# LayerNorm rows turned by transposing DMAs, and one 1/sqrt chain for two norms, in a gMLP block's z stage

## The chip, the cores and the metric

The kernel runs on one core of one Trainium2 chip. The metric is the time of one execution on the device in microseconds (us); several runs are made and their median is taken. The profile is of one execution, by the hardware profiler. Its engines are PE (TensorE's matmuls), PEld (TensorE's weight loads, which overlap PE), DVE (VectorE), ACT (ScalarE), POOL (GpSimd) and SP (SyncE, which issues DMAs; SPq is its queue). Each engine works through its instructions in the order of the program and waits on semaphores for others.

## The reference

One sequence of S = 2048 rows of D = 512, float32. First an attention block of 32 heads with a LayerNorm ahead of it, then a gMLP block with a LayerNorm ahead of it:

```python
x = A_x
h = x + _A_ref(_layernorm(x), A_wqkv, A_wo)
h2 = h + _B_ref(_layernorm(h), B_w_in, B_w_sp, B_b_sp, B_w_out)
...
z = _gelu(jnp.einsum("bsd,df->bsf", x, w_in))
z1 = z[..., :Fh]
z2 = _layernorm(z[..., Fh:], axis=-1)
g = jnp.einsum("ts,bsf->btf", w_sp, z2) + b_sp[None, :, None]
return jnp.einsum("bsf,fd->bsd", z1 * g, w_out)
```

Fh is 688. What is computed to the end of the z stage is h, then z from the LayerNorm of h, then the LayerNorm of z's second half.

## The kernel before, in words

The kernel has four stages: the projections q, k and v; attention (the longest by far), in which POOL also prepares the weights of what follows; the z stage; and the last stage with the spatial product and the output. Matmuls take float16 parts: a float32 tile is split into a float16 high part and a float16 rest, and `mm3` (lines 106 to 109) multiplies high by high, high by rest and rest by high.

The z stage works on 16 blocks of 128 rows in the order `h_rows`: 0, 1, 8, 9, 2, 10, 3, 11 and so on. Its loop over k (from line 1243) is written out by hand, under a manual schedule: the order in the code is the order on each engine. In iteration k it does this, for the block `sb` = row[k] and the later block `new` = row[k + 2]:

- `make_h(new)`: twelve matmuls (L747) of the attention's output o with wo. DVE adds x (L751, in the tile xr, which holds x and then h), SP stores h (L752), DVE takes statistics (L754).
- `split_o(row[k + 3])`: o's float16 high part on ACT (L737) and its rest on DVE (L740).
- `make_z(sb, 1, ...)`: two quarters of z, the second half of its columns, twelve matmuls each (lines 107 to 109) with hT, the turned LayerNorm of h, as the stationary operand; the Gelu on ACT (L1192).
- `turn(row[k + 1])`, between these two: PE transposes the float32 tile hn in four 128 × 128 blocks into PSUM (L1177), ACT takes the high part (L98), DVE the rest (L104).
- `scale_h(new)`: DVE makes 1/sqrt of the variance of h by three Newton steps (`rstd_of`, lines 111 to 131), and `minus_mean` (L768); ACT then makes hn (L1271).
- Statistics of z's second half (L1265), then two more quarters, the first half of z's columns.
- `gate_z(sb)`: z's first half is stored from ACT's queue (L1209); a second 1/sqrt chain on DVE; ACT normalizes z's second half (L1214); then float16 parts of it and of sums and differences of blocks, on ACT, POOL and DVE (L1196, L1197, L1220 to L1236). For k = 13 this is put off into the next iteration.
- `meanwhile()`, inside `gate_z`: POOL multiplies the next o by the reciprocals rc (L731), and SP asks for the o, rc and x of row[k + 5] (`load_o`: four o, four rc, one xr; L723, L726, L729).

In the last eight iterations SP also fetches operands of the last stage (L1163, op).

Pools set how far work can run ahead: accumulators `acc` of the z stage have five PSUM banks and the transposes two; xr and hn have three buffers, o and rc two; z's second half has four, its first half one. In the attention stage, h of the first two blocks is made between the units of the scores, at fixed values of n, and the LayerNorm of the first block on DVE (`new_hn`, L764).

Of the kernel before, what the change touches and what calls it, by code (L numbers as in the profile page):

```python
# [59 lines left out]
def block_kernel(ctx: ExitStack, tc: tile.TileContext, x, wqkv, wo, w_in, w_sp4, b_sp, w_out, out):  # L60
# [652 lines left out]
    wi4 = w_in.rearrange("(a p) c -> p a c", p=P)  # L713

    h_rows = [0, 1, HB, HB + 1] + [sb + HB * i for sb in range(2, HB) for i in range(2)]
    os_, o2s, xrs, hns, hTs = {}, {}, {}, {}, {}

    def load_o(sb):

        c = slice(sb * P, (sb + 1) * P)  # L720
        o = e2.tile([P, DB, P], F32, name="o")
        for d in range(DB):
            nc.sync.dma_start(o[:, d, :], o_scr[d, :, :DH, c])  # L723
        rc = e2.tile([P, DB, P], F32, name="rc")
        for d in range(DB):
            nc.sync.dma_start(rc[:, d, :], r_scr[8 * d:8 * d + 8, c].rearrange(  # L726
                "h (o s) -> h o s", o=1).to_broadcast([8, DH, P]))
        xrs[sb] = e2.tile([P, D], F32, name="xr", bufs=3)
        nc.sync.dma_start(xrs[sb], x[c, :])  # L729
        os_[sb] = o  # L730
        return lambda: nc.gpsimd.tensor_mul(o, o, rc)  # L731

# [27 lines left out]

    def new_hn(sb):
        mv, rs = scale_h(sb)
        hns[sb] = e2.tile([P, D], F32, name="hn", bufs=3)
        nc.vector.tensor_scalar(hns[sb], xrs.pop(sb), mv[:, 0:1], rs, op0=ALU.subtract, op1=ALU.mult)  # L764

    def minus_mean(pool, mv, rs):
        nb = pool.tile([P, 1], F32, name="nb")
# [20 lines left out]
    with ExitStack() as at:  # L788
# [256 lines left out]
        for n in range(0, len(units), 2):  # L1045
# [85 lines left out]
                invert()  # L1131
            if n in (474, 484, 504, 508):
                asked.append(load_o(h_rows[{474: 0, 484: 1, 504: 2, 508: 3}[n]]))
            if n in (484, 492, 508):
                asked.pop(0)()
            if len(later) == 1 or n in (498, 510):
# [2 lines left out]
                steps_h.append(make_h(h_rows[1], later[0].tile([P, 512], F32, name="h")))  # L1139
            if n == 502:  # L1140
                new_hn(h_rows[0])
        weigh(*prev)
        take(*prev[:2], e2)
        asked.append(load_o(h_rows[4]))
# [21 lines left out]
    with ExitStack() as mid:  # L1166
        m2 = mid.enter_context(tc.tile_pool(name="mid_2", bufs=2))
        zs, zst = {}, {}
        ps = mid.enter_context(tc.tile_pool(name="mid_ps", bufs=5, space=PSUM))
        pt = mid.enter_context(tc.tile_pool(name="mid_pt", bufs=2, space=PSUM))  # L1170

        def turn(sb):

            hn = hns.pop(sb)
            tp = pt.tile([P, DB, P], F32, name="tp")
            for d in range(DB):
                nc.tensor.transpose(tp[:, d, :], hn[:, d * P:(d + 1) * P], ident)  # L1177
            hTs[sb] = [m2.tile([P, DB, P], F16, name=f"hT{i}") for i in range(2)]
            split(hTs[sb][0], hTs[sb][1], tp, "act")

        def new_z(sb):
            zs[sb] = [m2.tile([P, FH], F32, name=f"z{i}", bufs=1 + 3 * i) for i in range(2)]
            zst[sb] = m2.tile([P, 2, 6], F32, name="zst")

        def make_z(sb, i, c):

            hT, f = hTs[sb], slice(i * FH + c * FC, i * FH + (c + 1) * FC)
            acc = ps.tile([P, 512], F32, name="acc")
            for d in range(DB):
                mm3(acc[:, :FC], hT[0][:, d, :], hT[1][:, d, :],  # L1190
                    wi2[0][:, d, f], wi2[1][:, d, f], d == 0, d == DB - 1)
            nc.scalar.activation(zs[sb][i][:, c * FC:(c + 1) * FC], acc[:, :FC], AF.Gelu_apprx_tanh,  # L1192
                                 scale=gelu_down)

        def parts(name, k, src, eh, el):
            (nc.gpsimd.tensor_copy if eh == "pool" else nc.scalar.copy)(T[name][0][:, k, :], src)  # L1196
            sub = lambda e: e.tensor_sub(T[name][1][:, k, :], src, T[name][0][:, k, :])  # L1197
            if el == "later":
                subs.append(sub)
            else:  # L1200
                sub(nc.gpsimd if el == "pool" else nc.vector)

        subs, put_off = [], []

        def gate_z(sb, meanwhile):

            z = zs.pop(sb)
            rows = slice(sb * P, (sb + 1) * P)
            nc.scalar.dma_start(z_scr[rows, :], z[0])  # L1209
            mv = m2.tile([P, 2], F32, name="zmv")  # L1210
            nc.vector.bn_aggr(mv, zst.pop(sb))
            rs = rstd_of(m2, mv[:, 1:2], 1, up=Z2_UP)
            nb = minus_mean(m2, mv, rs)
            nc.scalar.activation(z[1], z[1], AF.Identity, bias=nb, scale=rs)  # L1214
            zs[sb] = z[1]
            meanwhile()
# [12 lines left out]
            t2 = m2.tile([P, FC], F32, name="t2", bufs=1)  # L1229
            e.tensor_sub(t2, b22, t1)  # L1230
            parts("t2", k, t2, eh, el)
            parts("b22", k, b22, "pool" if last else "act", "pool")
            nc.gpsimd.tensor_sub(b12, b22, b12)
            parts("t3", k, b12, "pool", "pool")
            parts("b21", k, b21, "pool" if last else "act", "pool" if last else "later")
            nc.gpsimd.tensor_sub(t2, b21, t2)  # L1236
            parts("n4", k, t2, "pool", "pool")

        row = dict(enumerate(h_rows))
        with tc.manual_schedule(engines={E.PE, E.Activation, E.DVE, E.Pool, E.SP}):  # L1240
            asked.pop(0)()
            turn(row[0])
            new_hn(row[1])
            for k in range(NB):
                sb, new = row[k], row.get(k + 2)
                if new is not None:
                    for _ in make_h(new, ps.tile([P, 512], F32, name="acc")):
                        pass
                if k + 3 < NB:
                    split_o(row[k + 3])  # L1250
                new_z(sb)
                make_z(sb, 1, 0)
                if k + 1 < NB and k != NB - 2:
                    turn(row[k + 1])
                if new is not None:
                    mv, rs = scale_h(new)
                    nb = minus_mean(e2, mv, rs)
                if subs:
                    subs.pop()(nc.vector)
                make_z(sb, 1, 1)  # L1260
                if k == NB - 2:
                    turn(row[k + 1])
                    put_off.pop()()
                for c in range(2):
                    nc.vector.bn_stats(zst[sb][:, c, :], zs[sb][1][:, c * FC:(c + 1) * FC])  # L1265
                make_z(sb, 0, 0)
                make_z(sb, 0, 1)
                hTs.pop(sb)
                if new is not None:
                    hns[new] = e2.tile([P, D], F32, name="hn", bufs=3)  # L1270
                    nc.scalar.activation(hns[new], xrs.pop(new), AF.Identity, bias=nb, scale=rs)  # L1271
                if k == 1:
                    invert()
                if k >= NB - 8:
                    ask()

                def meanwhile(k=k):
                    if k + 4 < NB:
                        asked.pop(0)()
                    if k + 5 < NB:  # L1280
                        asked.append(load_o(row[k + 5]))

                if k == NB - 3:
                    put_off.append(lambda sb=sb, then=meanwhile: gate_z(sb, then))
                else:
                    gate_z(sb, meanwhile)
    early.close()
    late.close()

# [314 lines left out]
```

## Time and profile before

| | |
|---|---|
| median of 3 runs | 1714.83 us (1714.73 to 1715.37) |
| span of the profiled execution, first to last instruction | 1712.3 us |
| PE busy | 1699.5 us, 99% |
| DVE busy | 1452.5 us, 85% |
| ACT busy | 1317.5 us, 77% |
| POOL busy | 813.6 us, 48% |
| z stage on PE | 1294.45 to 1451.57 us |

The page gives no time of the profiled execution other than its span. In rows of the profile, L12 is line 12 of the kernel; `out<-in` are tiles by their names, `x12` a count; a bracket holds the idle time of that engine ahead of the row and what ended it. A row of the timeline begins with the start and the duration in us. In the table of waits the numbers are the total, the count and the longest.

### The profile page before, as it was taken

To read this page: it belongs to the slowest core of one execution; us is meant where nothing else is said; L and a number is where in the kernel's file an instruction comes from. 1 tells how busy PE (TensorE), PEld (TensorE's weight loads), DVE (VectorE), ACT (ScalarE), POOL (GpSimd) and SP (SyncE) were. 2 spreads that over 40 slices of the span, in tenths; PEclk is the share of its full clock that TensorE was granted. 3 is DMA by queue.
4 is the path that set the end of the run, shared out by engine and by line. 5 is a ranking of instruction groups with operands and counts; after the bars stand their busy time and mean duration, and the time that the engine had idled before them with its cause. 6 is when DMAs were issued, how large, how long until landed. Compare 5 with 4: busy or idle time off the path is not lost.

```text
span 1712.3 us, 36689 instructions
## 1 busy us (share of the span) xinstructions
PE 1699.5 (99%) x13508; PEld 644.7 (38%) x13508; DVE 1452.5 (85%) x3051; ACT 1317.5 (77%) x2584; POOL 813.6 (48%) x1062
## 2 busy tenths in 40 slices
PE   9999999999999999999999999999999999999999
PEld 4533222222222222222222222222225666656665
DVE  7688999999999999999999999999936787543444
ACT  4334999999999999999999999999995545211111
POOL 1231867776673267687767776400002766300100
PEclk9999999999999999999999999999999999999999
DMA  5534332342221244344434444300114454664551
GB/s 185 167 94 144 103 89 68 101 94 82 81 68 25 56 118 117 104 144 125 130 113 124 132 140 130 80 13 19 37 39 124 140 173 140 233 234 156 198 217 44
DMA packets 189309, 196.03 MB, mean 114 GB/s; under 512 B 67496, under 2 KB 140008, under 8 KB 189128
## 3 DMA queue, kind: packets, MB, share of 16 engines
q1 hardware_dynamic: 186824, 188.04, 36.8%
q10 hardware_dynamic: 2304, 5.64, 0.8%
q8 instruction: 106, 1.74, 0.4%
q14 instruction: 75, 0.61, 0.1%
HBM read 122.10 MB, written 65.93 MB: 110 GB/s over the span
## 4 chain that ended last, share of the span: by engine, by line
PE 78%; DVE 12%; DMA 3%; POOL 2%; ACT 2%; SPq 2%; issue 1%; ACTq 0%; POOLq 0%; DVEq 0%
PE pv L830 26%; PE s L805 17%; PE m L223 9%; DVE mx L228 7%; PE acc L107 4%; PE g L108 4%; PE g L109 4%; PE g L107 4%; PE acc L109 4%; PE acc L108 4%; DMA rc<-r_scr 1%; DVE ab L237 1%; DVE og L840 1%; SPq L723 1%; DVE rs_t L124 1%
## 5 line engine op out<-in xcount | busy, mean ns | idle before, releaser
L814 ACT ACTIVATE pt<-s 128x512 f32<-128x512 f32 x1968 | 1006.2, 637 | 5.5 <-PE m L223 4.3
L228 DVE TENSOR_REDUCE mx<-m 128x1 f32<-128x512 f32 x1510 | 947.5, 682 | 11.7 <-PE m L223 2.9
L805 PE MATMUL s<-qst,kst 50*128 50x512 f16 x2048 | 604.2, 379 | 0.2
L830 PE MATMUL pv<-pt,vst 128*32 128x256 f32 (+1 forms) x6056 | 598.1, 466 | 4.1 <-DVE og L840 1.3
L223 PE MATMUL m<-kst,qst 48*128 48x512 f16 x1510 | 452.4, 381 | 0.0
L805 PEld LDWEIGHTS <-kst 50*128 50x128 f16 x2048 | 132.0, 94 | 352.1 <-issue 323.7
L830 PEld LDWEIGHTS pv<-pt,vst 128*32 128x32 f32 x6056 | 119.5, 108 | 290.7 <-issue 277.3
L223 PEld LDWEIGHTS <-qst 48*128 48x128 f16 x2048 | 159.2, 93 | 173.6 <-issue 124.2
L223 PE MATMUL m<-uvs,qst 48*128 48x512 f16 x504 | 190.5, 380 | 0.6 <-DVE mx L228 0.6
L245 POOL TENSOR_SCALAR nm<-nm 128x16 f32<-128x16 f32 x32 | 6.6, 206 | 358.8 <-DVE nm L242 358.8
L237 DVE CUSTOM_DVE_ANT_0 ab<-m,ab 128x512 f32<-128x512 f32 x252 | 170.5, 677 | 2.7 <-ACT ab L233 2.7
L233 ACT ACTIVATE ab<-m 128x512 f32<-128x512 f32 x252 | 157.3, 624 | 15.5 <-PE m L223 14.8
L1368 ACT ACTIVATE pr<-pr,up 128x304 f32<-128x304 f32 (+1 forms) x32 | 17.0, 574 | 109.2 <-DVE up L1322 109.2
L991 POOL TENSOR_TENSOR op<-raw,op 128x512 f16<-128x512 f32 x80 | 92.9, 1161 | 6.0
L914 POOL TENSOR_TENSOR raw<-raw 128x512 f32<-128x512 f32 (+1 forms) x84 | 83.3, 991 | 6.7
L919 POOL TENSOR_TENSOR acc_sp<-acc_sp,raw 128x512 f32<-128x512 f32 x63 | 80.4, 1277 | 4.5
L109 PE MATMUL acc<-wi,hT 128*128 128x344 f16 x256 | 79.1, 309 | 0.3 <-DVE hT L104 0.3
L107 PE MATMUL acc<-wi,hT 128*128 128x344 f16 x256 | 79.1, 309 | 0.0
L108 PE MATMUL acc<-wi,hT 128*128 128x344 f16 x256 | 79.1, 309 | 0.0
L1510 POOL TENSOR_TENSOR pr<-pr,z 128x344 f32<-128x344 f32 x8 | 7.3, 914 | 145.9 <-DMA whole<-squares 108.3
L911 POOL TENSOR_SCALAR raw<-raw 128x512 f32<-128x512 f32 (+1 forms) x88 | 52.3, 594 | 19.7 <-DMA raw<-in_wqkv 12.4
L1509 DVE TENSOR_TENSOR pr<-g,v 128x344 f32<-128x344 f32 x8 | 4.1, 517 | 66.6 <-PE g L109 63.5
(247 smaller groups left out, 2292.9 us busy)
## 6 DMA issues: line engine op xcount, KB each, us to landing
raw<-in_w_sp SPq DMA_DIRECT2D x128, 256.0 KB
s_scr<-op SPq DMA_DIRECT2D x64, 256.0 KB
op<-s_scr SPq DMA_DIRECT2D x32, 512.0 KB
a_scr<-op SPq DMA_DIRECT2D x48, 256.0 KB
op<-a_scr SPq DMA_DIRECT2D x24, 512.0 KB
o_scr<-og SPq DMA_DIRECT2D x64, 128.0 KB
qst<-q_scr SPq DMA_DIRECT2D x192, 32.0 KB
kst<-k_scr SPq DMA_DIRECT2D x48, 128.0 KB
```

Source lines behind the costliest of these rows:

```text
L107: nc.tensor.matmul(ps, lh, rh, start=first, stop=False, **kw)
L108: nc.tensor.matmul(ps, lh, rl, start=False, stop=False, **kw)
L109: nc.tensor.matmul(ps, ll, rh, start=False, stop=last, **kw)
L223: nc.tensor.matmul(acc, q[r, p, c], keys[r, p], start=True, stop=True)
L228: nc.vector.reduce_max(at(t, e if t else e - 1), acc, axis=AX.X)
L233: nc.scalar.activation(ab[0], acc, AF.Abs)
L237: nc.vector.tensor_tensor_reduce(ab[0], acc, ab[0], 0.5, LOW, ALU.add, ALU.max, at(0, 0))
L805: nc.tensor.matmul(s, kst[hg % 2][r, p, kb * P:(kb + 1) * P], qst[hg * NQ + qb][r, p, :], start=True, stop=True)
L814: nc.scalar.activation(pts[p, kb][:, t, :], s, AF.Exp, scale=scales_[hg // 2])
L830: nc.tensor.matmul(pv[0][32 * j:32 * j + 32, a:b], vst[hg % 2][:, c:c + 32], pts[j % 2, kb][:, j // 2, a:b], start=kb == 0, stop=kb == NB - 1,
L914: pool.tensor_mul(got[0] if n else acc, got[0], got[0])
L991: chores.append((lambda: pool.tensor_sub(t[0][:, 1], of(), t[0][:, 0]), TT))
```

## The change

The turn of hn leaves PE. ACT (or, for the first block, DVE) makes the float16 high part of hn while hn lies in rows (`halve_h`), DVE makes the rest (`turn_h`), both into one tile hp of 128 × 1024, and SP turns this by one transposing DMA of 256 KB into hT. The two PSUM banks of the transposes go to the accumulators. The first block's is done in the attention stage, after n = 504.

`scale_both` takes the place of `scale_h` and the chain in `gate_z`: the variances of z's second half (block `sb`) and of h (block `new`) stand in two columns, and one chain of Newton steps works on both. hn of row[k + 1] is made at the head of iteration k, from the chain of iteration k − 1, and so is the normalization of z2 of row[k − 1]. The split of o stands ahead of that normalization. x's rows are asked by a call of their own (`load_row`), ahead of o's. z's first half is stored right after its last Gelu. The case put off at k = 13 is gone.

```diff
+    def load_row(sb):
+        xrs[sb] = e2.tile([P, D], F32, name="xr", bufs=3)
+        nc.sync.dma_start(xrs[sb], x[sb * P:(sb + 1) * P, :])
...
-        xrs[sb] = e2.tile([P, D], F32, name="xr", bufs=3)
-        nc.sync.dma_start(xrs[sb], x[c, :])
...
-        hns[sb] = e2.tile([P, D], F32, name="hn", bufs=3)
+        hns[sb] = e2.tile([P, D], F32, name="hn")
...
+    def halve_h(sb, on_act=True):
+        hps[sb] = e2.tile([P, 2, D], F16, name="hp")
+        if on_act:
+            nc.scalar.activation(hps[sb][:, 0], hns[sb], AF.Copy)
+        else:
+            nc.vector.tensor_copy(hps[sb][:, 0], hns[sb])
+
+    def turn_h(sb):
+        hp = hps.pop(sb)
+        nc.vector.tensor_sub(hp[:, 1], hns.pop(sb), hp[:, 0])
+        t = e2.tile([P, 2 * DB, P], F16, name="hT")
+        nc.sync.dma_start_transpose(t, hp.rearrange("p i c -> p (i c)"))
+        hTs[sb] = [t[:, :DB], t[:, DB:]]
...
+            if n == 504:
+                halve_h(h_rows[0], False)
+                turn_h(h_rows[0])
...
-        ps = mid.enter_context(tc.tile_pool(name="mid_ps", bufs=5, space=PSUM))
-        pt = mid.enter_context(tc.tile_pool(name="mid_pt", bufs=2, space=PSUM))
-        def turn(sb):
-            hn = hns.pop(sb)
-            tp = pt.tile([P, DB, P], F32, name="tp")
-            for d in range(DB):
-                nc.tensor.transpose(tp[:, d, :], hn[:, d * P:(d + 1) * P], ident)
-            hTs[sb] = [m2.tile([P, DB, P], F16, name=f"hT{i}") for i in range(2)]
-            split(hTs[sb][0], hTs[sb][1], tp, "act")
+        ps = mid.enter_context(tc.tile_pool(name="mid_ps", bufs=7, space=PSUM))
...
+        def scale_both(new, sb):
+            n = 1 if new is None else 2
+            mv = m2.tile([P, 2, 2], F32, name="mv2")
+            hv = m2.tile([P, 2], F32, name="hv2")
+            for i, (row, stats, up) in enumerate(((sb, zst, Z2_UP), (new, hst, HN_UP))[:n]):
+                nc.vector.bn_aggr(mv[:, i, :], stats.pop(row))
+                nc.vector.tensor_scalar(hv[:, i:i + 1], mv[:, i, 1:2], EPS, 0.5 / up ** 2,
+                                        op0=ALU.add, op1=ALU.mult)
+            r, t, nb = [m2.tile([P, 2], F32, name=f"{i}_2")[:, :n] for i in ("r", "t", "nb")]
...
+            for _ in range(3):
+                nc.vector.tensor_mul(t, r, r)
+                nc.vector.tensor_mul(t, t, hv)
+                nc.vector.scalar_tensor_tensor(r, t, 1.5, r, op0=ALU.subtract, op1=ALU.mult)
+            nc.vector.scalar_tensor_tensor(nb, mv[:, :n, 0], -1.0, r, op0=ALU.mult, op1=ALU.mult)
...
-            nc.scalar.dma_start(z_scr[rows, :], z[0])
-            mv = m2.tile([P, 2], F32, name="zmv")
-            nc.vector.bn_aggr(mv, zst.pop(sb))
-            rs = rstd_of(m2, mv[:, 1:2], 1, up=Z2_UP)
-            nb = minus_mean(m2, mv, rs)
+            z, (nb, rs) = zs.pop(sb), scaled.pop(sb)
...
-            turn(row[0])
             new_hn(row[1])
+            halve_h(row[1])
+            turn_h(row[1])
             for k in range(NB):
                 sb, new = row[k], row.get(k + 2)
+                if k and k + 1 < NB:
+                    nb, rs = scaled.pop(row[k + 1])
+                    hns[row[k + 1]] = e2.tile([P, D], F32, name="hn")
+                    nc.scalar.activation(hns[row[k + 1]], xrs.pop(row[k + 1]), AF.Identity, bias=nb, scale=rs)
+                    halve_h(row[k + 1])
+                    turn_h(row[k + 1])
+                if k + 4 < NB:
+                    asked.pop(0)()
                 if new is not None:
                     for _ in make_h(new, ps.tile([P, 512], F32, name="acc")):
                         pass
                 if k + 3 < NB:
                     split_o(row[k + 3])
+                if k + 4 < NB:
+                    load_row(row[k + 4])
+                if k + 5 < NB:
+                    asked.append(load_o(row[k + 5]))
+                if k >= NB - 8:
+                    ask()
+                if k:
+                    gate_z(row[k - 1])
                 new_z(sb)
                 make_z(sb, 1, 0)
-                if k + 1 < NB and k != NB - 2:
-                    turn(row[k + 1])
-                if new is not None:
-                    mv, rs = scale_h(new)
-                    nb = minus_mean(e2, mv, rs)
                 if subs:
                     subs.pop()(nc.vector)
                 make_z(sb, 1, 1)
...
+                scale_both(new, sb)
                 make_z(sb, 0, 0)
                 make_z(sb, 0, 1)
+                nc.scalar.dma_start(z_scr[sb * P:(sb + 1) * P, :], zs[sb][0])
...
-                    gate_z(sb, meanwhile)
+            gate_z(row[NB - 1])
```

The order on DVE in a middle iteration of the z loop, before; st and zst are the statistics of h and z, mv and zmv their means and variances, rs_v to rs_u the chain:

```order
L126 TENSOR_SCALAR rs_u<-rs_t_21602,rs_u 128x1
L768 TENSOR_SCALAR nb<-rs_u,zmv 128x1
L751 SCALAR_TENSOR_TENSOR xr<-acc,fig_1845,xr 128x512
L754 BN_STATS st<-xr 128x6
L740 SCALAR_TENSOR_TENSOR o_21659<-o,fig_1844,o_21658 128x512
L104 TENSOR_TENSOR hT_21685<-tp,hT_21684 128x512
L758 BN_AGGR mv<-st 128x2
L114 TENSOR_SCALAR rs_v_21690<-mv 128x1
L116 TENSOR_SCALAR rs_r_21692<-rs_v_21690 128x1
L124 TENSOR_SCALAR rs_t_21694<-rs_r_21692,rs_v_21690 128x1
```

The same place after the change:

```order
L1234 SCALAR_TENSOR_TENSOR r_21453<-t_21454,r_21453 128x2
L1235 SCALAR_TENSOR_TENSOR nb_21455<-mv_21447,r_21453 128x2
L780 TENSOR_TENSOR hp<-hn,hp 128x512
L754 SCALAR_TENSOR_TENSOR xr<-acc,fig_1845,xr 128x512
L757 BN_STATS st<-xr 128x6
L743 SCALAR_TENSOR_TENSOR o_21522<-o,fig_1844,o_21521 128x512
L1210 TENSOR_TENSOR b_1_20670<-z_21415,b_0_20669 128x344
L1303 BN_STATS zst<-z_21552 128x6 x2
L1224 BN_AGGR mv_21585<-zst 128x2
L1225 TENSOR_SCALAR hv_21586<-mv_21585 128x1
L1224 BN_AGGR mv_21585<-st 128x2
```

The rest of hn (hp) stands first after the chain, where h's own chain stood later in the iteration; one chain follows the statistics of z.

The order of SP's DMAs in a later iteration, before:

```order
L752 DMA h_scr<-xr 128x512
L1163 DMA op<-a_0_scr 128x2048
L723 DMA o<-o_scr 128x1x128 x4
L726 DMA rc<-r_scr 128x1x128 x4
L729 DMA xr<-in_x 128x512
```

And after:

```order
L782 DMA_TRANSPOSE hT<-hp 128x8x128
L755 DMA h_scr<-xr 128x512
L721 DMA xr<-in_x 128x512
L728 DMA o<-o_scr 128x1x128 x4
L731 DMA rc<-r_scr 128x1x128 x4
L1186 DMA op<-a_0_scr 128x2048
```

The transposing DMA stands at the head of an iteration, and x's rows have moved ahead of o's.

More of the change, by code (lines that the diff above doesn't have):

```diff
@@ L715, in block_kernel @@
     h_rows = [0, 1, HB, HB + 1] + [sb + HB * i for sb in range(2, HB) for i in range(2)]
-    os_, o2s, xrs, hns, hTs = {}, {}, {}, {}, {}
+    os_, o2s, xrs, hns, hps, hTs = {}, {}, {}, {}, {}, {}
+    def load_row(sb):
+        xrs[sb] = e2.tile([P, D], F32, name="xr", bufs=3)
+        nc.sync.dma_start(xrs[sb], x[sb * P:(sb + 1) * P, :])
     def load_o(sb):
@@ L1133, in block_kernel @@
                 asked.append(load_o(h_rows[{474: 0, 484: 1, 504: 2, 508: 3}[n]]))
+                load_row(h_rows[{474: 0, 484: 1, 504: 2, 508: 3}[n]])
             if n in (484, 492, 508):
@@ L1201, in parts, with gate_z @@
                 sub(nc.gpsimd if el == "pool" else nc.vector)
[L1203 to L1208, printed above, removed]
-            nc.scalar.dma_start(z_scr[rows, :], z[0])
-            mv = m2.tile([P, 2], F32, name="zmv")
-            nc.vector.bn_aggr(mv, zst.pop(sb))
-            rs = rstd_of(m2, mv[:, 1:2], 1, up=Z2_UP)
-            nb = minus_mean(m2, mv, rs)
+        subs = []
+        def scale_both(new, sb):
[7 more added lines that the diff above has]
+            r, t, nb = [m2.tile([P, 2], F32, name=f"{i}_2")[:, :n] for i in ("r", "t", "nb")]
+            hv = hv[:, :n]
+            nc.vector.tensor_scalar(r.bitcast(I32), hv.bitcast(I32), -0.5, GUESS,
+                                    op0=ALU.mult, op1=ALU.add)
+            for _ in range(3):
[3 more added lines that the diff above has]
+            nc.vector.scalar_tensor_tensor(nb, mv[:, :n, 0], -1.0, r, op0=ALU.mult, op1=ALU.mult)
+            for i, row in enumerate((sb, new)[:n]):
+                scaled[row] = nb[:, i:i + 1], r[:, i:i + 1]
+        scaled = {}
+        def gate_z(sb):
+            z, (nb, rs) = zs.pop(sb), scaled.pop(sb)
             nc.scalar.activation(z[1], z[1], AF.Identity, bias=nb, scale=rs)
             zs[sb] = z[1]
-            meanwhile()
             if sb < HB:
@@ L1260, in block_kernel @@
                 make_z(sb, 1, 1)
-                if k == NB - 2:
-                    turn(row[k + 1])
-                    put_off.pop()()
                 for c in range(2):
                     nc.vector.bn_stats(zst[sb][:, c, :], zs[sb][1][:, c * FC:(c + 1) * FC])
+                scale_both(new, sb)
                 make_z(sb, 0, 0)
                 make_z(sb, 0, 1)
+                nc.scalar.dma_start(z_scr[sb * P:(sb + 1) * P, :], zs[sb][0])
                 hTs.pop(sb)
-                if new is not None:
-                    hns[new] = e2.tile([P, D], F32, name="hn", bufs=3)
-                    nc.scalar.activation(hns[new], xrs.pop(new), AF.Identity, bias=nb, scale=rs)
                 if k == 1:
                     invert()
[L1274 to L1285, printed above, removed]
-                    gate_z(sb, meanwhile)
+            gate_z(row[NB - 1])
     early.close()
```

## The prediction

> **What bounds the kernel now.** I read the page's head, then the stretches of the z stage (the loop that makes z from h, one iteration for each block of 128 rows), then the timeline of TensorE and the table of waits there.
>
> ```profile
> span 1712.3 us, 36689 instructions
> 1304.47:1344.58 40.11, 40.11 (x259) 25.37 (x257) 28.84 (x93) 20.50 (x36) 21.82 (x25) 1.00 0.49 146
> 1344.58:1426.50 81.92, 81.73 (x515) 49.97 (x513) 67.41 (x213) 42.62 (x77) 56.43 (x65) 1.00 0.52 158
> 1426.50:1451.60 25.10, 24.84 (x167) 15.98 (x165) 19.15 (x67) 13.63 (x26) 14.44 (x19) 1.00 0.34 124
> ```
>
> The columns are the stretch, its length, then busy time of PE, PEld, DVE, ACT and POOL, the clock, the DMA share and GB/s. PE is busy for 81.73 of 81.92 us at clock 1.00: the stage ends with PE, and the other engines matter only when they are late for it. DVE is next with 67.41 us, and its dead time between small operations is not in that.
>
> ```profile
> 1294.45 2.75 PE L747 MATMUL acc<-wo,o 128*128 128x512 f16 x12 [0.22 <-DVE og L840]
> ...
> 1426.50 2.75 PE L747 MATMUL acc<-wo,o 128*128 128x512 f16 x12
> ...
> 1429.09 0.31 PE L107 MATMUL acc<-wi,hT 128*128 128x344 f16 x1
> ...
> 1430.84 0.60 PE L1177 MATMUL tp<-ident,hn 128*128 128x128 f32 x4
> 1431.27 0.31 PE L107 MATMUL acc<-wi,hT 128*128 128x344 f16 x1
> ...
> 1451.57 0.31 PE L107 MATMUL g<-b,op 128*128 128x344 f16 x1
> ```
>
> From starts: h of one block (12 matmuls) holds PE for 1429.09 − 1426.50 = 2.59 us. A quarter of z (12 matmuls) holds it for 1430.84 − 1429.09 = 1.75 us, the whole z for 7.00. The four transposes hold it for 1431.27 − 1430.84 = **0.43 us**. The stage runs from 1294.45 to 1451.57, 157.12 us.
>
> **The terms.** The new program's PE has 14 h's and 16 z's there: 14 × 2.59 + 16 × 7.00 = 148.26 us. The difference, **8.86 us**, is 15 sets of transposes (6.45 us; the sixteenth lay ahead of 1294.45) and 2.41 us of waits:
>
> ```profile
> PEld L747 <- DVE o L740: 2.3, 5, 0.6
> PEld tp L1177 <- ACT hn L1271: 1.7, 6, 0.3
> PE acc L109 <- DVE hT L104: 0.3, 1, 0.3
> ```
>
> These name 4.3 us at the weight load; a part is covered by the matmul still running, so I use 2.41. All three waits lose their place. The transposes are gone. The split of o stands at the head of an iteration and is used in the next one's h, some 4 us later by the arithmetic below. What takes their place is one wait: z needs a transposing DMA to have landed.
>
> **The chain that feeds that DMA.** Let T be the start of an iteration's h on PE, and E the end of the shared 1/sqrt chain. The chain's parts on DVE:
>
> ```profile
> 7.98 0.16 DVE L129 TENSOR_TENSOR rs_t<-rs_r 128x4 f32<-128x4 f32 x1
> 8.18 0.16 DVE L130 TENSOR_TENSOR rs_t<-rs_t,rs_v 128x4 f32<-128x4 f32 x1
> ...
> 1410.22 0.92 DVE L1265 BATCH_NORM_STATS2 zst<-z 128x6 f32<-128x344 f32 x2
> 1411.18 0.21 DVE L1211 BATCH_NORM_AGGREGATE zmv<-zst 128x2 f32<-128x12 f32 x1
> ...
> 1413.47 0.21 DVE L768 TENSOR_SCALAR nb<-rs_u,zmv 128x1 f32<-128x1 f32 x1
> 1413.60 0.74 DVE L751 SCALAR_TENSOR_TENSOR xr<-acc,fig,xr 128x512 f32<-128x512 f32 x1
> 1414.38 0.69 DVE L754 BATCH_NORM_STATS2 st<-xr 128x6 f32<-128x512 f32 x1
> ```
>
> A chain of ten takes 1413.60 − 1411.18 = 2.42 us today, and there are two of them per iteration. Multiplies of a few columns come 0.20 us apart (8.18 − 7.98). The shared chain has 15 operations, so 15 × 0.20 = 3.0 us against 4.8. Two columns are not in the trace; 0.16 for four and 0.15 for one hold them from both sides.
>
> Half of z's second part leaves PE at T + 2.59 + 3.50 = 6.09. I add 0.2 until ACT starts, 0.55 for the Gelu (row below), half of the 0.92 statistics and 3.0 for the chain: T + 10.3, some 0.8 us into the next iteration. Then ACT and DVE:
>
> ```profile
> 1409.39 0.81 ACT L1271 ACTIVATE hn<-xr,nb,rs_u 128x512 f32<-128x512 f32 x1 [1.83 <-DVE nb L768]
> 1413.72 0.96 ACT L1214 ACTIVATE z<-z,nb,rs_u 128x688 f32<-128x688 f32 x1 [3.52 <-DVE nb L768]
> 1415.10 0.72 ACT L737 ACTIVATE o<-o,fig 128x512 f16<-128x512 f32 x1
> 1415.72 0.53 ACT L1192 ACTIVATE z<-acc,fig 128x344 f32<-128x344 f32 x1
> 1416.77 0.69 DVE L104 TENSOR_TENSOR hT<-tp,hT 128x512 f16<-128x512 f32 x1
> ```
>
> hn 0.81, then its float16 half 0.72 (not in the trace; o's has the same shape and memory; the rows here, 0.53 to 0.81, bound it), then the rest 0.69 on DVE: with handovers E + 2.35, that is T + 3.15. SP then issues the transpose. z of that block starts at T + 9.59 + 2.59 = T + 12.18. **The DMA has 9.0 us** in a steady iteration. It has less in two places. For the last block no h stands ahead: z starts at T + 7.00, which leaves 3.85 us. For the second block SP is late:
>
> ```profile
> 1298.24 2.43 SPq L726 DMA_DIRECT2D rc<-r_scr  x4
> 1300.76 0.40 SPq L729 DMA_DIRECT2D xr<-in_x  x1
> 1301.21 1.39 SPq L850 DMA_DIRECT2D sums<-o_scr  x2
> ```
>
> Without the xr issue, the transpose leaves SP at about 1302.15, and PE wants z of that block at 1294.45 + 12.18 = 1306.63: 4.5 us. So with L from issue to landing the gain is 8.86 − (L − 4.5) − (L − 3.85), each bracket not below zero, as long as L is under 9.0.
>
> **The price L** of 256 KB, SBUF to SBUF, transposed: the trace has no such DMA. Bounds:
>
> ```profile
> 0.75 1.81 SPq L286 DMA_DIRECT2D xg<-in_x  x4
> 3.25 0.69 DVE L385 BATCH_NORM_STATS2 st<-xg 128x6 f32<-128x512 f32 x1 [2.11 <-DMA xg<-in_x]
> ...
> 1672.19 10.67 SPq L1397 DMA_DIRECT2D whole<-squares  x16
> 1684.26 1.58 ACT L1403 ACTIVATE pT<-whole 128x768 f16<-128x768 f32 x2 [5.52 <-DMA whole<-squares]
> ...
> 1322.88 7.05 DMA o<-o_scr
> 1409.90 5.17 DMA rc<-r_scr
> ```
>
> From below: a plain 256 KB load lands 3.25 − 0.75 = 2.5 us after its issue. From above: the longest landing in the chain of waits, 7.05. In between, the only SBUF-to-SBUF traffic: 768 KB in 16 issues takes 10.67 us and lands 1.40 after the last; a third of it is 3.56 + 1.40 = 5.0. I take **L = 5.0**, the nearest kind, and the rc loads ahead of it in the queue, 5.17 to land, agree with it; the DMA engines are at half share (0.52 above), so the extra bytes find room. Gain: 8.86 − 0.5 − 1.15 = **7.2 us**.
>
> A rule of the Trainium skill speaks against the change. "VectorE: DVE Perf Modes", The three transpose paths, gives 390 ns for a 128 × 128 block on TensorE and 1309 ns by DMA, and advises TensorE. The trace has 0.43 us for four blocks of float32 on PE, cheaper than the 390 ns apiece. By 8 × 1.309 = 10.5 us, an estimate from that page of the Trainium skill, L would pass the 9.0 us.
>
> **What else moves, at nothing.** ACT swaps the split of hT for that of hn. DVE loses 1.8 us per iteration. z_scr leaves one iteration's tail earlier. In the attention stage block 0's halves and transpose lie between units of the scores, well ahead of their use at 1297; they push SP's next o load back by the one issue, which is read only by the split in the first iteration. On SP each iteration issues the transpose, h_scr, xr, four o and four rc (and one op in the later half): twice 2.43, three times 0.4 and the transpose, under 9.59 unless that one issue takes over 3.5 us; h_scr behind it is read only in the last stage. The normalization of z2 moves an iteration later, with PSUM for seven tiles where an iteration uses five, so that PE need not wait for a late Gelu. At the stage's end POOL and ACT have two products, 7 us of PE, before row 15's parts are needed, as now.
>
> **Rivals.** *DVE becomes the bound.* Its loop is E, 1.64 until hn's half is there, then the rest 0.61 to the next start, xr 0.78, st 0.69, o 0.75, statistics 0.96, chain 3.0: 8.4 us. Every second iteration has the b subtraction:
>
> ```profile
> 1409.27 1.02 DVE L1197 TENSOR_TENSOR b<-z,b 128x344 f16<-128x344 f32 x1
> 1448.33 0.51 DVE L1197 TENSOR_TENSOR b<-z,b 128x344 f16<-128x344 f32 x1
> ```
>
> It takes 0.51 or, beside POOL, 1.02. If the rest of hn doubled likewise, the loop is 9.1 and 10.1 in turn, 9.6 on average: PE's 9.59. At 10.1 throughout, 13 × 0.5 = 6.6 us are lost: 1714.2. Against it: it needs POOL at every collision. 6%.
>
> *The DMA is slow but fits*, L of 6.9 to 9.3: 7.05 gives 8.86 − 2.55 − 3.2 = 3.1 us, time 1711.7; about 8.6 gives nothing. 9%.
>
> *Slower: the DMA takes the eight blocks one behind the other.* Above L = 9.0 every z waits. From one E to the one two iterations on lie 2.35 + L + 7.8 (half of z, Gelu, statistics, chain), so an iteration is (10.15 + L)/2. At eight of the small SBUF issues, each about 2.07 from issue to landing (10.67/16 + 1.40), L = 16.5: 13.3 us an iteration, 12 × 3.7 = 45 us lost and some 24 at the two ends, less 8.86: about 1775. It decides from L = 8.6. For it: nothing shows this operation. Against: the 7.05. 15%. By the Trainium skill's 10.5 us it would be 10.3 an iteration: 8.86 − 6.0 − 6.65 − 12 × 0.73, some 12.6 us slower, 1727.
>
> *The change doesn't do what it says* would be the 2.41 us of waits staying: 4.8 us of gain, 1710.0, inside the forecast's own case.
>
> **The numbers.** The profiled execution's span of 1712.3 would be 1705.1. The timed median, 1714.83, is 2.53 above that span; I keep the 2.53: **1707.6 us**. The forecast (gain 3.5 to 8.9) has 70%. Its own range is 1705.5 to 1711.4; taking in the slow DMA and the DVE loop, 1705.5 to 1714.5. Faster by over 0.2% (3.4 us, about what a measurement of this kernel can tell from no change) 72%: the forecast and a third of the DVE case. Within it 13%, slower 15%.
>
> **What would show it.** No transposes on PE and h to h 9.59 us apart where 10.02 or more stands now; E about 0.8 us after h starts; a wait of z's matmuls for the DMA only at the second and the last block, 0.5 and 1.2 us; the chain 3.0 us on DVE. Wrong would be a wait for hT in every iteration (L over 9), or PE waiting for nothing and still more than 9.6 apart (the DVE loop, through late Gelus).

## The result, and the profile after

| | us, median (lowest to highest) | runs |
|---|---|---|
| before | 1714.83 (1714.37 to 1715.44) | 5 |
| after | 1724.94 (1723.52 to 1726.17) | 5 |

The ratio is **1.0058, 95% interval 1.0047 to 1.0069**: 10 us slower, where 7.2 us faster was forecast. The profiled execution of after took 1724.94 us, with a span of 1723.2. Against before's 1712.3 the span grew by 10.9 us, and 9.7 of these lie in the z stage, which TensorE now runs from 1295.86 to 1462.71: 166.85 us against 157.12.

The stretches of the stage in after, with the columns of the prediction's first view (stretch, length, busy time of PE, PEld, DVE, ACT and POOL, clock, DMA share, GB/s):

```profile
1295.86:1324.63 28.77, 28.77 (x180) 17.61 (x180) 17.94 (x58) 14.45 (x23) 6.82 (x7) 1.00 0.67 150
1324.63:1344.45 19.82, 19.36 (x123) 11.66 (x121) 15.72 (x40) 9.12 (x16) 12.54 (x16) 1.00 0.60 165
1344.45:1434.17 89.72, 79.91 (x483) 46.67 (x481) 73.17 (x175) 45.08 (x81) 56.85 (x67) 0.98 0.68 169
1434.17:1462.71 28.54, 24.10 (x159) 15.04 (x157) 20.84 (x61) 14.15 (x26) 19.10 (x25) 1.00 0.51 152
```

In the first stretch TensorE never stands still: three blocks in 28.77 us, 9.59 each, as the sum of matmuls said. In the third it is idle for 9.8 of 89.72 us. Note POOL: 6.82 us of 28.77 in the good stretch, 56.85 of 89.72 in the bad one.

TensorE's timeline in after shows what it waits for:

```profile
1305.45 2.75 PE L750 MATMUL acc<-wo,o 128*128 128x512 f16 x12
1315.04 2.75 PE L750 MATMUL acc<-wo,o 128*128 128x512 f16 x12
1324.63 2.75 PE L750 MATMUL acc<-wo,o 128*128 128x512 f16 x12
...
1347.21 2.33 PE L750 MATMUL acc<-wo,o 128*128 128x512 f16 x10 [2.17 <-DVE o L743]
...
1380.95 4.02 PE L750 MATMUL acc<-wo,o 128*128 128x512 f16 x10 [2.22 <-DVE o L743]
...
1427.16 0.32 PE L107 MATMUL acc<-wi,hT 128*128 128x344 f16 x1 [1.27 <-DMA hT<-hp]
...
1434.17 2.75 PE L750 MATMUL acc<-wo,o 128*128 128x512 f16 x12
```

From 1324.63 to 1434.17 lie ten blocks: 10.95 us each. TensorE waits in some blocks for the split of o (L743, VectorE) and in others for hT. Both are made behind VectorE's chain. The row at 1380.95 also took 4.02 us for ten matmuls that take 2.33 at 1347.21. The longest wait of the stage, 3.16 us for hT, is at 1447.08, the z of block k = 14.

VectorE's groups in the stage (1294 to 1463) in after, shapes kept apart (busy us, mean ns of one | idle before), and one chain of it while POOL is idle and one while POOL works:

```profile
L1232 DVE TENSOR_TENSOR t<-r 128x2 f32<-128x2 f32 x42 | 17.1, 407 | 1.4
L1234 DVE SCALAR_TENSOR_TENSOR r<-t,r 128x2 f32<-128x2 f32 x42 | 15.2, 361 | 1.5
L1233 DVE TENSOR_TENSOR t<-t,hv 128x2 f32<-128x2 f32 x42 | 12.3, 292 | 1.5
L1229 DVE TENSOR_SCALAR r<-hv 128x2 int32<-128x2 int32 x14 | 6.3, 453 | 0.5
L1225 DVE TENSOR_SCALAR hv<-mv 128x1 f32<-128x1 f32 x30 | 4.6, 154 | 1.0
```
```profile
1303.30 0.21 DVE L1224 BATCH_NORM_AGGREGATE mv<-zst 128x2 f32<-128x12 f32 x1
...
1304.22 0.16 DVE L1232 TENSOR_TENSOR t<-r 128x2 f32<-128x2 f32 x1
1304.41 0.16 DVE L1233 TENSOR_TENSOR t<-t,hv 128x2 f32<-128x2 f32 x1
...
1305.98 0.16 DVE L1235 SCALAR_TENSOR_TENSOR nb<-mv,r 128x2 f32<-128x2 f32 x1
...
1349.18 0.21 DVE L1224 BATCH_NORM_AGGREGATE mv<-zst 128x2 f32<-128x12 f32 x1
...
1350.41 0.83 DVE L1232 TENSOR_TENSOR t<-r 128x2 f32<-128x2 f32 x1
...
1352.01 0.69 DVE L1233 TENSOR_TENSOR t<-t,hv 128x2 f32<-128x2 f32 x1
1352.74 0.83 DVE L1234 SCALAR_TENSOR_TENSOR r<-t,r 128x2 f32<-128x2 f32 x1
...
1354.35 0.69 DVE L1235 SCALAR_TENSOR_TENSOR nb<-mv,r 128x2 f32<-128x2 f32 x1
```

POOL's timeline in after, beside the second of these:

```profile
1349.51 0.84 POOL L1210 TENSOR_TENSOR b<-z,b 128x344 f16<-128x344 f32 x1
1350.31 0.92 POOL L1262 TENSOR_TENSOR z<-z,z 128x344 f32<-128x344 f32 x1
1351.29 0.48 POOL L1209 CAST t<-z 128x344 f16<-128x344 f32 x1
1351.85 0.84 POOL L1210 TENSOR_TENSOR t<-z,t 128x344 f16<-128x344 f32 x1
1352.64 0.91 POOL L1265 TENSOR_TENSOR t<-z,t 128x344 f32<-128x344 f32 x1
```

Read side by side: the operation at 1350.41 ends at 1351.24, POOL's of 0.92 us at 1351.23. The next long one, at 1352.01, ends at 1352.70, POOL's of 0.84 at 1352.69; the one after it at 1353.57, POOL's of 0.91 at 1353.55. Each long operation of the chain ends where an operation of POOL ends: it has stood still until then. So do all 66 operations of the stage's chains that took over 0.25 us: each ends within 0.03 us of the end of an operation of POOL. The same operation takes 0.16 us while POOL is idle. From the start of the statistics' merge to the shift's end the first chain takes 1306.14 − 1303.30 = 2.84 us, the other 1355.04 − 1349.18 = 5.86. Of the 14 chains of two columns two take 2.8 us, three 3.5 to 3.6, and nine between 5.4 and 6.3. One column wide beside POOL, L1225 stays at 154 ns; it has one tensor to read. Width alone does not spare an operation: in the last two chains, which are one column wide, the multiplies of two tensors stood up to 0.83 us.

The four slow groups are busy for 50.9 us. At 0.16 us apiece these 140 operations would take 22.4: some 28 us over the stage, 2.0 for each of 14 chains. The shift L1235 ends at 1330.38 in the third chain and ten iterations later at 1441.40: VectorE's loop is 11.1 us, over TensorE's 9.59.

The split of o, which TensorE waits for by name, also stood still. It takes 0.73 or 0.74 us in most blocks. Ahead of the waits of 2.17 and 2.22 us it took the times below, beside POOL's multiplication of the next o (L734, from 1345.35 to 1346.61 at the first). So some 1.0 us of each of these two waits is its own:

```profile
1345.35 1.81 DVE L743 SCALAR_TENSOR_TENSOR o<-o,fig,o 128x512 f16<-128x512 f32 x1
...
1379.18 1.71 DVE L743 SCALAR_TENSOR_TENSOR o<-o,fig,o 128x512 f16<-128x512 f32 x1
```

**Theory T1**: the chain of two-column operations is held up by POOL, makes VectorE's loop the bound, and both of TensorE's waits follow from it. **Rival T2**: the transposing DMA is itself late, and the rest follows. A variant, **T2'**: ScalarE, not VectorE, delays the next h. ScalarE's timeline in after, at one block, shows z_scr's issue on its queue and the next h's normalization behind it, after 3.77 us of idle time that an o load ended:

```profile
1319.18 0.33 ACTq L1307 DMA_DIRECT2D z_scr<-z  x1
1319.56 0.82 ACT L1279 ACTIVATE hn<-xr,nb,r 128x512 f32<-128x512 f32 x1 [3.77 <-DMA o<-o_scr]
```

### The profile page after: what moved, and what is told of

It is laid out like the page before. It is cut to its first block, busy times and chain, and to the rows that moved or that the text cites. A ratio compares the mean times of both kernels' runs of the same rounds, so it can differ in the third digit from the quotient of the medians.

```text
span 1723.2 us, 36527 instructions
## 1 busy us (share of the span) xinstructions
PE 1696.3 (98%) x13444; PEld 637.3 (37%) x13444; DVE 1457.4 (85%) x2988; ACT 1320.1 (77%) x2583; POOL 810.4 (47%) x1062
## 4 chain that ended last, share of the span: by engine, by line
PE 78%; DVE 14%; DMA 3%; SPq 2%; ACT 1%; POOL 1%; issue 1%; ACTq 0%; DVEq 0%; POOLq 0%
PE pv L849 26%; PE s L824 18%; PE m L223 9%; DVE mx L228 7%; PE g L107 4%; PE g L109 4%; PE g L108 4%; PE acc L107 4%; PE acc L109 4%; PE acc L108 4%; DMA rc<-r_scr 2%; DVE ab L237 1%; DVE og L859 1%; SPq L728 1%; DVE o L743 1%
## 5 line engine op out<-in xcount | busy, mean ns | idle before, releaser
L734 POOL TENSOR_TENSOR o<-o,rc 128x512 f32<-128x512 f32 x16 | 20.4, 1274 | 110.9 <-DMA rc<-r_scr 59.6
```

## The experiments

All are made from after, with the kernel before timed beside them on the same chip; the ratios are to that.

### e_psum: the chain's working value in PSUM

```diff
+            ch = pc.tile([P, 8], F32, name="chain")
+            r = ch[:, :n]
...
-            r, t, nb = [m2.tile([P, 2], F32, name=f"{i}_2")[:, :n] for i in ("r", "t", "nb")]
...
-            for _ in range(3):
-                nc.vector.tensor_mul(t, r, r)
-                nc.vector.tensor_mul(t, t, hv)
-                nc.vector.scalar_tensor_tensor(r, t, 1.5, r, op0=ALU.subtract, op1=ALU.mult)
-            nc.vector.scalar_tensor_tensor(nb, mv[:, :n, 0], -1.0, r, op0=ALU.mult, op1=ALU.mult)
+            for i in range(3):
+                nc.vector.tensor_mul(t, r, hv)
+                nc.vector.tensor_mul(t, t, r)
+                nc.vector.scalar_tensor_tensor(rs if i == 2 else r, t, 1.5, r, op0=ALU.subtract, op1=ALU.mult)
+            for i, row in enumerate((sb, new)[:n]):
+                nc.vector.tensor_scalar(nb[:, i:i + 1], rs[:, i:i + 1], mv[:, i, 0:1], -1.0, op0=ALU.mult, op1=ALU.mult)
```

pc is a PSUM pool of one bank; hv and t stay in SBUF, as hv_p and t_p.

> The changed kernel, with the shared 1/sqrt chain's working value r in PSUM, so that each two-column operation of two tensors reads one operand from PSUM and one from SBUF (the last Newton step writes SBUF again; the two shifts are one-column operations). T1 (the chain of two-column operations is slowed by GpSimd's work, to 5.4 us instead of 3, and makes VectorE's loop 11.1 us, above the 9.59 us of TensorE's work): if the slowing needs two operands in SBUF, the chain falls to 3.0 to 3.5 us, VectorE's loop to about 9 us, the unhindered distance of 9.59 us holds through the steady blocks, and the time is 1708 to 1712 us. T2 (the transposing DMA comes too late by itself): the waits for hT stay, 1720 to 1725 us.

Measured: 1711.39 us (10 runs), ratio **0.9986** (0.9976 to 0.9996), by the two ratios some 12 us below after. The stage's stretch and VectorE's groups in e_psum:

```profile
1294.90:1450.19 155.29, 149.45 (x936) 91.04 (x936) 103.10 (x355) 84.19 (x144) 98.00 (x116) 1.00 0.74 174
```
```profile
L1236 DVE TENSOR_TENSOR t_p<-chain,hv_p 128x2 f32<-128x2 f32 x42 | 6.7, 160 | 1.4
L1237 DVE TENSOR_TENSOR t_p<-t_p,chain 128x2 f32<-128x2 f32 x42 | 6.6, 157 | 1.5
L1238 DVE SCALAR_TENSOR_TENSOR chain<-t_p,chain 128x2 f32<-128x2 f32 x28 | 4.6, 166 | 1.0
L1233 DVE TENSOR_SCALAR chain<-hv_p 128x2 int32<-128x2 int32 x14 | 2.3, 164 | 0.5
```

The same count of Newton operations of the same shapes: 157 to 166 ns on average where they took 292 to 407, and the integer guess 164 for 453. What is changed about them is that one operand, or the guess's result, lies in PSUM. (The first product is now r times hv in place of r times r; L1233, of two different tiles, was slowed in after all the same.) POOL works beside them as before: 98.00 us in the stage, 95.31 in after's (the four stretches above). Every one of the 14 chains now takes 2.98 to 3.00 us, the prediction's figure. T1 is borne out and T2 falls: with the DMAs untouched, the stage lasts 155.29 us. (No run takes POOL's work away. That it is POOL which the operations wait for rests on the 66 ends above and on this run.) It is not the forecast's 149.9 yet; TensorE still waits for hT, 0.56 us in block k = 3 and 0.90, 1.50 and 2.09 in k = 10 to 12.

### e_short: without the Newton steps

```diff
-            for _ in range(3):
+            for _ in range(0):
```

> The changed kernel without the three Newton steps (9 of the chain's 13 two-column operations left out; the 1/sqrt is the first guess alone). T1: the chain takes 1.2 to 2 us, VectorE's loop falls to some 7.5 us, o is split in time and hT asked in time: 1706 to 1711 us. T2 (the transposing DMA's own latency is what TensorE waits for): 1720 to 1725 us.

Measured: 1709.87 us (10 runs), ratio 0.9980 (0.9970 to 0.9990). The chain takes 1.07 to 2.65 us, where 1.2 to 2 were expected, with the slowing that is left in the operations that remain. This agrees with T1 and not with T2. That all the Newton steps could be left out for only 1.5 us against e_psum says that VectorE is no longer the bound there; TensorE's last wait for hT of 1.97 us is in this kernel too.

### e_const: no wait for a later transposing DMA

```diff
         nc.sync.dma_start_transpose(t, hp.rearrange("p i c -> p (i c)"))
-        hTs[sb] = [t[:, :DB], t[:, DB:]]
+        hTc.append(t)
+        hTs[sb] = [hTc[0][:, :DB], hTc[0][:, DB:]]
```

> The changed kernel, with every transposing DMA issued as before but the z of all blocks computed from the first block's hT, so that TensorE waits for no later transposing DMA (the z of the other blocks is left out). T1: VectorE's loop stays at 11 us, TensorE waits for the split o instead: 1719 to 1724 us. T2: the waits go with hT, 1707 to 1712 us.

Measured: 1725.40 us (4 runs), ratio 1.0068 (1.0051 to 1.0085): 1.4 us above T1's range and far from T2's, as slow as after with every wait for hT gone. The table of waits of e_const in the stage (us in total, times, longest):

```profile
ACT hn L1280 <- DVE nb L1236: 61.3, 12, 8.0
...
PEld L750 <- DVE o L743: 11.4, 6, 3.2
...
PE g L107 <- POOL b L1211: 4.9, 1, 4.9
```

In after the second row has 8.9 us, and TensorE waits 0.7 us for POOL at the stage's end, where the third row has 4.9. What TensorE no longer waits for hT, it waits for the split of o and, at the end, for POOL's parts of the normalized z, which are made behind VectorE's last chains.

### e_cols: two one-column chains

```diff
+            for i, (row, stats, up, pool) in enumerate(((sb, zst, Z2_UP, m2), (new, hst, HN_UP, e2))[:n]):
+                mv = pool.tile([P, 2], F32, name="mvc")
+                nc.vector.bn_aggr(mv, stats.pop(row))
+                rs = rstd_of(pool, mv[:, 1:2], 1, up=up)
+                scaled[row] = minus_mean(pool, mv, rs), rs
```

> The changed kernel, with two one-column chains one behind the other (2 times the 2.42 us that one took in the kernel before) in the place of the shared two-column chain. T1: the chains take 4.9 us and no longer depend on what GpSimd does, against 5.4 of the shared one: VectorE's loop is 10.4 to 10.6 us, 1717 to 1721 us, a little faster than the changed kernel. If the shared chain were the cheap one of the two: slower than the changed kernel, 1727 us or more. T2: no difference, 1723 to 1726 us.

Measured: 1721.45 us (4 runs, 1719.32 to 1724.31), ratio 1.0050 (1.0033 to 1.0067). The groups in the stage of e_cols:

```profile
L124 DVE TENSOR_SCALAR rs_t<-rs_u,rs_v 128x1 f32<-128x1 f32 x62 | 16.9, 273 | 2.2
L126 DVE TENSOR_SCALAR rs_u<-rs_t,rs_u 128x1 f32<-128x1 f32 x62 | 13.3, 214 | 2.2
```

One column wide, with the second factor as an operand of one value per row, they take 273 and 214 ns each, as in the kernel before, and both chains together 4.89 or 4.90 us in every one of 14 blocks. The durations are as expected; the time is 0.5 us above its upper end, and by the ratios (1.0050 and after's 1.0058, whose intervals overlap) it can't be told from after. The stage of the profiled execution, one of 1719.39 us, is 162.80 us, 4 below after's: if there is a difference, it is a gain. So two chains of 4.9 us together cost no more than one "shorter" chain of 5.4 to 6.3: beside POOL the merging, counted as 1.8 us saved per block, saved nothing.

### f_psum_zsp and f_zsp: z_scr's write from SyncE

```diff
                     turn_h(row[k + 1])
+                if k:
+                    put_z(row[k - 1], nc.sync)
...
-                nc.scalar.dma_start(z_scr[sb * P:(sb + 1) * P, :], zs[sb][0])
+                zout[sb] = zs[sb][0]
```

`put_z` issues the same write from the engine that it is given. The last block's stays on ScalarE.

> The chain with r in PSUM, and z_scr's write issued by SyncE behind the next block's transposing DMA, no more by ScalarE ahead of the next h's normalization. T2' (with the chain mended, what still makes hT late in blocks 10 to 12 is ScalarE, which stands at z_scr's issue until an older o load has landed, 4.1 us in two places, and normalizes the next h behind it): those waits of 1 to 2 us go, nearly every distance is 9.59 us, and the time falls another 3 to 6 us, to 1705 to 1708 us. If the transposing DMA is late there because the queue is full (the loads of the last stage's operands begin in the same blocks): no change from 1711 us.

> The changed kernel with only z_scr's write moved to SyncE; the chain stays in SBUF. T1 (VectorE's loop of 11.1 us is the bound): the next h is normalized when its scale is ready, as in most blocks before, and the loop stays: 1721 to 1725 us. T2' alone: 1712 to 1716 us.

Measured: f_psum_zsp 1708.39 us (7 runs), ratio **0.9973** (0.9961 to 0.9984); f_zsp 1723.84 us (5 runs), ratio 1.0065 (1.0051 to 1.0078). The row of waits that this is about in e_psum, the longest of ScalarE in f_psum_zsp, and the latter's stage:

```profile
ACT hn L1283 <- DMA o<-o_scr: 26.2, 7, 4.2
```
```profile
ACT z L1206 <- DMA z_scr<-z: 47.9, 13, 6.2
```
```profile
1294.31:1446.02 151.71, 149.13 (x936) 91.09 (x936) 101.38 (x355) 82.45 (x144) 97.78 (x115) 1.00 0.72 178
```

In e_psum the next h's normalization stands behind z_scr's issue on ScalarE's queue, seven times, for 26.2 us, until an o load has landed. Moved to SyncE, that wait is gone and the stage falls from 155.29 to 151.71 us (one execution each; by the two ratios the time falls by some 2.2 us). Alone, without the mended chain, it brings nothing that can be measured (f_zsp against after): T2' is real but second, since while VectorE is late ScalarE waits for it anyway (61.0 us for the shift in after, 12 times). The expectation of 1705 to 1708 was missed by 0.4 us. The second row has a likely reason, which the next experiment takes up: there is one buffer for z's first half, so the next Gelu now waits until the write has landed, up to 6.2 us, with the next h's normalization behind it.

### g_psum_zsp2: a second buffer for z's first half

```diff
-            zs[sb] = [m2.tile([P, FH], F32, name=f"z{i}", bufs=1 + 3 * i) for i in range(2)]
+            zs[sb] = [m2.tile([P, FH], F32, name=f"z{i}", bufs=2 + 2 * i) for i in range(2)]
```

> As f_psum_zsp, with a second buffer for the half z0 of z, so that ScalarE's activation of the next z0 need not wait until z_scr's write has landed (13 waits, 47.9 us in all, up to 6.2 us in f_psum_zsp), behind which the next h's normalization stands in order. If these waits are what still makes hT late in blocks 10 to 12 (TensorE waits of 0.7 to 0.8 us there): they go, the z stage falls from 151.7 to about 150 us, 0.9955 to 0.9975 of the kernel before. If the transposing DMA is late there because its queue is full: as f_psum_zsp, 0.9973.

Measured: **1707.23 us** (5 runs, 1706.95 to 1707.57), ratio **0.9966** (0.9952 to 0.9979), faster than both kernels; from f_psum_zsp's time it can't be told, since the intervals overlap. The stage and TensorE's only wait for hT in g_psum_zsp2:

```profile
1294.41:1444.95 150.54, 148.59 (x936) 91.42 (x936) 104.44 (x355) 86.81 (x144) 100.66 (x116) 1.00 0.72 180
```
```profile
1413.55 0.32 PE L107 MATMUL acc<-wi,hT 128*128 128x344 f16 x1 [1.30 <-DMA hT<-hp]
```

TensorE is busy for 148.59 of 150.54 us, at clock 1.00; the distances are 9.59 in every block but that one. The 13 waits of ScalarE for z_scr are gone, but the last of the waits that they were to explain, in k = 12, is not (0.76 us in f_psum_zsp, 1.30 here): there the transposing DMA itself came late (see L below). VectorE is busy for 104.44 us where after needed 127.68 over its longer stage.

### f_psum_pe and g_psum_pe: the transposes back on TensorE

Both take the chain in PSUM and z_scr on SyncE, and turn h with the code of the kernel before. In g_psum_pe z's first half has two buffers, and the turned h has the place in memory that it has with the DMA.

```diff
-                    halve_h(row[k + 1])
-                    turn_h(row[k + 1])
...
                 make_z(sb, 1, 0)
+                if k + 1 < NB:
+                    turn(row[k + 1])
```

> As f_psum_zsp, but with the four transposes of each h on TensorE and the split of the transposed h on ScalarE and VectorE, as in the kernel before, so that the transposing DMAs alone are undone. If the transposing DMAs save what they take from TensorE (16 times 0.43 us) and bring no waits: 1712 to 1715 us, 6 to 7 us above f_psum_zsp. If they gave part of it back: 2 to 5 us above f_psum_zsp or less.

> As g_psum_zsp2 with the four transposes of each h on TensorE, and the place in memory of the transposed h as with the DMA, so that the first load of the last stage (raw_w) is not held up until the last z_scr has landed, as it was in f_psum_pe (8.4 us). The distances stay 10.02 us and the z stage about 155 us; if that held-up load was the whole loss of f_psum_pe against its stage: 1709 to 1713 us; if not: 1718 to 1721 us again.

Measured: f_psum_pe 1720.67 us (5 runs), ratio 1.0045 (1.0031 to 1.0059), outside its expectation; g_psum_pe 1711.16 us (11 runs), ratio 0.9987 (0.9978 to 0.9996). Both run the stage in 154.84 and 154.83 us with 10.02 or 10.03 from block to block. What f_psum_pe lost lies behind the stage. There the first load of the last stage's weights, raw_w, stood still:

```profile
SPq L1524 <- DMA z_scr<-z: 8.4, 1, 8.4
```

TensorE then stood 6.53 us at 1470.11, ahead of its first matmuls on these weights.

In g_psum_pe raw_w is asked for at 1450.02 instead of 1459.42, TensorE has no such wait, and the time is 9.5 us less. So the transposing DMAs alone are worth 154.83 − 150.54 = 4.3 us of the stage, and some 3.6 us of time by the two ratios (0.21% of 1713), against 6.45 for the transposes that they take off TensorE.

## Why the prediction was wrong

**TensorE's terms: right.** No transposes are left on TensorE, and where nothing hinders it blocks follow each other by 9.59 us. The floor of 148.26 us for the matmuls stands: 148.59 in g_psum_zsp2.

**The failed step: "The shared chain has 15 operations, so 15 × 0.20 = 3.0 us against 4.8."** It measured 5.4 to 6.3 us in most blocks. The rows from which it was taken are at 7.98 and 8.18 us, where POOL does nothing, as before's stretch there and VectorE's line L130 in all its runs show:

```profile
7.90:9.00 1.10, 1.10 (x7) 0.49 (x5) 0.90 (x7) 0.88 (x3) 0.00 (x0) 1.00 1.05 402
```
```profile
L130 DVE TENSOR_TENSOR rs_t<-rs_t,rs_v x12: 161/161/1005, 8.2 to 59.6; 128x4 f32<-128x4 f32 x12
```

POOL's busy time in that stretch is 0.00. The second view has the shortest, the median and the longest of twelve: one of them took 1005 ns. In before's trace it runs from 26.01 to 27.01 beside an operation of POOL from 25.84 to 27.00 (L319). It was the sign that this form can stand still, and I priced by the median. "Two columns are not in the trace; 0.16 for four and 0.15 for one hold them from both sides" bounded the work and not the waiting: what sets it is which operands lie in SBUF and what POOL does, as e_psum shows.

**E, right where POOL is idle.** "Some 0.8 us into the next iteration" (its own sum gives 10.3 − 9.59 = 0.7): the first two chains end at 1306.14 and 1315.71, 0.7 us behind the starts of h at 1305.45 and 1315.04. The third ends 5.75 us behind 1324.63.

**The rival "DVE becomes the bound": the right mechanism, mispriced.** I gave it 6% and 1714.2, since it had only the rest of hn and b double beside POOL. In after the rest of hn never did (691 to 694 ns in all 15), while the chain, held at 3.0, did. With 5.4 to 6.3 in place of 3.0, its loop of 8.4 comes to 10.8 to 11.7, and 11.1 was measured. TensorE's side of it: 166.85 − 152.14 = 14.7 us idle in the stage, and 3.9 us more busy time than the 148.26 of its matmuls, a part of it at a clock below 1.00. The sign that I named, "PE waiting for nothing and still more than 9.6 apart", was not how it looked; TensorE waited by name, for o and hT.

**"The split of o stands at the head of an iteration and is used in the next one's h, some 4 us later":** on VectorE it stands behind the chain, and came up to 2.2 us too late: by the same step, and in the two worst blocks by 1.0 us of its own standing beside POOL, which was not priced either.

**A move kept at nothing.** "z_scr leaves one iteration's tail earlier" stood under that heading; on ScalarE's queue it costs 155.29 − 151.71 = 3.6 us of the stage once the chain is mended, and the single buffer behind it another 1.2 (151.71 − 150.54), each from one execution.

**L: the size about right, its place not.** From SyncE's issue to the waiting z it was 4.7 to 6.0 us in after and 3.4 at the end, against 5.0. In g_psum_zsp2 at the block that still waits it was 1413.55 − 1405.51 = 8.0, issued behind four o, four rc and a load for the last stage. There the two waits forecast, 0.5 at the second block and 1.15 at the last, did not come; one of 1.30 at k = 12 did. The rivals "the DMA is slow" and "the eight blocks one behind another" did not decide anything.

**A place left out.** The prediction gives the DMA less than 9.0 us in two places. There is a third: block k = 14 has no h ahead of its z either, which leaves 9.59 − 3.15 = 6.4 us. At L = 5.0 that costs nothing, but TensorE's longest wait in after, 3.16 us, was there. The range's lower end is also off: a gain of 8.9 us gives 1705.9, not 1705.5.

With the chain and ScalarE's order mended and a second buffer, the change gives 1707.2 us, 6.0 below the kernel before on the same chip (1713.23), where 7.2 were forecast. That this is near the 1707.6 forecast is in part chance. It speaks for the sum of matmuls, and not for the prediction.

## What to carry to other kernels

Price a small operation beside what the other engines will be doing, from a row in that stage; where a view gives shortest, median and longest, a longest of six times the median is a rival with a price. Before merging two short serial chains into one wider one, see where their operands lie: two chains whose operations never stand still (4.9 us here) can be as cheap as one that does (5.4 to 6.3). And a DMA issued from a computing engine's queue is an instruction in that queue: what waits there holds up the arithmetic behind it (26.2 us in e_psum).

## What the runs showed of the hardware

- A VectorE operation of one or two columns with both tensors in SBUF, 0.16 us alone, took up to 1.14 us beside POOL (L1233 at 1325.80 in after) and ended with POOL's operation; with one of the tensors in PSUM it never did (e_psum, two columns: means of 157 to 166 ns). The Trainium skill, "SBUF — State Buffer", Who interferes with whom, says so: an instruction with two SBUF inputs contends with a GpSimd instruction that reads SBUF, and one with at most one such input, outside certain modes, does not. These runs agree on both halves.
- Where VectorE's operation had begun first, POOL's took longer: the rest of hn, with both tensors in SBUF, kept its 0.69 us in all 15 blocks of after, and four casts of POOL that met it took 0.92 us where 0.48 is usual.
- The integer guess, one tensor in and one out in SBUF, collides two columns wide (453 ns on average) and not one wide (154 ns in after, 153 in all 31 of e_cols); with its result in PSUM it does not either (164 ns). The Trainium skill, "VectorE: DVE Perf Modes", What auto-detection actually checks, has the condition: an operation with one tensor enters the mode 2×_2P, which uses both read ports, where source and result are in SBUF and their outermost dimensions longer than one are both even or equal. The two rows of two columns agree with it. I had not expected the place of the result to matter.
- A DMA transposing 128 × 1024 float16 in SBUF was used by a waiting TensorE 3.4 us after its issue with little around it (after) and 8.0 us after it in a loaded queue (g_psum_zsp2). SyncE was held 1.24 to 2.79 us by the issue (after). In the stage the first queue carried 34252 packets in after for 18376 in before, some 1000 more for each of 15 transposes.
- Why a write issued by ScalarE waits for an o load that it doesn't read, the traces don't say; moved to SyncE, the wait was gone from ScalarE (26.2 us in e_psum, none in f_psum_zsp).
- Behind one of TensorE's waits in after, of 2.22 us, the granted clock was 0.58 on average over 1380.95 to 1384.97, and ten matmuls took 4.02 us where 2.33 are usual. Behind the waits of 2.17 and 3.16 us the matmuls ran as usual, at 1.00. What sets the one apart from the others, the runs don't show.
